# Two edits to the load queues of a decode kernel: x on ScalarE's queue, and W_down's last 96 rows in eight loads

## The chip, the core and the metric

The kernel runs on one core of one Trainium2 chip. The metric is the device time of one execution in microseconds (us). Three runs of the kernel before gave 670.46, 670.48 and 671.56; the median is 670.48. The profile and the trace are of a further execution, which took 671.36.

## The reference, cut to what matters

One new token per sequence, two sequences, model width 512. An attention block with a cache of 8192 positions and 32 heads of 128, then a gated feed-forward block of width 1376, each behind a layer norm and with a residual:

```
q      = layernorm(x) @ wq                       # x (2,1,512), wq (512, 4096)
scores = q . k_cache / sqrt(128)                 # k_cache (2, 32, 8192, 128), bf16
o      = softmax(scores) . v_cache
h      = x + o @ wo                              # wo (4096, 512)
gate, up = layernorm(h) @ W_gate, layernorm(h) @ W_up     # (512, 1376) each
out    = h + (relu(gate) * up) @ W_down          # W_down (1376, 512)
```

The two caches are 268 MB of the 281 MB that are read. Everything is read once.

## The kernel before, in words

**Steps.** The attention runs in N = 32 steps (line 108); a step is one sequence and two heads. Step i needs K(i) and V(i), 4 MB each (4096 KB in the profile), loaded by `load_kv` (lines 111 to 118). There are two buffers for K and two for V, so K(i) and K(i+2) share one, as do V(i) and V(i+2). In a step, TensorE transposes and multiplies a quarter of K (`scores_pe`, lines 248 to 278), VectorE multiplies the rest with q (`products`, line 286) and adds it up by halves (`scores`, lines 301 and 305), ScalarE takes the exponentials (line 320), and TensorE multiplies them with V one step later (`values`, line 336; `values_cols`, line 359, in the last two steps). `behind` normalises finished groups of heads and multiplies them with W_o.

**Order of the loads.** The order is the program's own (`tc.manual_schedule()`, line 138); no planner moves anything. All 85 loads and stores are issued by SyncE (SP), one after another: x (line 141), W_q (line 142), K(0) in four pieces, K(1), V(0) (lines 143 to 145), W_o in four pieces (lines 195 to 201), and then in the loop over steps (lines 413 to 444): K(i+2) as soon as `scores(i)` has read its buffer, V(i+1) as soon as `values(i-1)` has read its own. In step 8 (line 429) come three loads of W_down's last 96 rows, 64, 24 and 8 rows, into the last block of the tile `wd_sb`. In step 30 come W_gate, W_up and the rest of W_down (lines 435 to 444). So around line 432 SP's order is K(10), V(9), the W_down rows, K(11), V(10), K(12), V(11).

**What SP waits for.** Besides the buffers there is a second kind of wait, which no line of the kernel shows. The framework hands each load one of eight completion semaphores in turn, named DMAHW0 to DMAHW7 in the built program, and a load that gets a semaphore must wait until the load that had it before, eight loads earlier, has landed. Most of these waits are long fulfilled, or are those for the buffer anyway.

**Start.** x is cast by VectorE (line 168) and goes through a layer norm (`ln_cols`, lines 120 to 136) to `xn`; 128 small matmuls with W_q give q (line 176). ScalarE begins with loading an activation table and a warm-up activation (line 165).

**End.** After the last step come the residual (line 454), the second layer norm, gate and up (line 463), `hm` (line 473), the product with W_down, the last 96 rows first (line 478), and the store (line 484).

Of the kernel before, what the change touches and what calls it, by code (L numbers as in the profile page):

```python
# [13 lines left out]
def _free(t, offset, dims):  # L14

    return bass.AP(tensor=t.tensor, offset=t.offset + offset, ap=[t.ap[0]] + [list(d) for d in dims])


def _dram(t, offset, dims):
    return bass.AP(tensor=t.tensor, offset=t.offset + offset, ap=[list(d) for d in dims])  # L20
# [3 lines left out]
def kernel(  # L24
# [13 lines left out]
    nc = tc.nc  # L38
    P = nc.NUM_PARTITIONS
    B, Sq, D = A_x.shape  # L40
    _, Hkv, Sk, Dh = A_k_cache.shape
    Hq = A_wq.shape[1] // Dh
    F = B_W_gate.shape[1]
    KC = D // P
# [16 lines left out]
    FC = 11  # L61
# [17 lines left out]
    wd_sb = big.tile([P, FC, D], bf16)  # L79
# [31 lines left out]
    def load_kv(cache, buf, i, pieces=1):  # L111
        b, g = steps[i]
        w = ROW // pieces
        for k in range(pieces):
            nc.sync.dma_start(
                out=buf[:, i % 2, k * w:(k + 1) * w],
                in_=_dram(cache, (b * Hkv + 2 * g) * Sk * Dh + k * w, [[ROW, P], [1, w]]),
            )
# [19 lines left out]
    with tc.manual_schedule():  # L138

        xb = small.tile([P, B, KC], bf16, tag="xb")  # L140
        nc.sync.dma_start(out=xb, in_=_dram(A_x, 0, [[KC, P], [D, B], [1, KC]]))
        nc.sync.dma_start(out=wbig, in_=_dram(A_wq, 0, [[KC * Hq * Dh, P], [1, KC * Hq * Dh]]))
        load_kv(A_k_cache, kbuf, 0, pieces=4)
        load_kv(A_k_cache, kbuf, 1)
# [7 lines left out]
            out=nscale, in_=nscale, compare_op=ALU.not_equal, fill=-SCALE,  # L152
# [7 lines left out]
            out=pick, in_=pick, compare_op=ALU.not_equal, fill=1.0,  # L160
# [13 lines left out]
        for h in range(Hq):  # L174
            for c in range(KC):
                nc.tensor.matmul(  # L176
                    out=q_ps[:, h, :], lhsT=wq_sb[:, c, h * Dh:(h + 1) * Dh], rhs=xn[:, c, :],
# [4 lines left out]
        for b in range(B):  # L182
            for g0 in range(0, NG, 4):
                r_ps = ps2.tile([P, 4, Dh], f32, tag="tp")
                for k in range(4):
                    for j in range(2):
                        nc.tensor.matmul(
                            out=r_ps[j * HALF:(j + 1) * HALF, k, :],
# [6 lines left out]
        for h0, n in SETS:  # L195
            nc.sync.dma_start(
                out=wbig[:, h0 * D:(h0 + n) * D], in_=_dram(A_wo, h0 * Dh * D, [[n * D, P], [1, n * D]]),
            )
        nc.sync.dma_start(
            out=wo_sb[:, HM:Hq, :], in_=_dram(A_wo, HM * Dh * D, [[D, P], [Dh * D, Hq - HM], [1, D]]),  # L200
        )
        for (h0, n), qu, re in zip(SETS, quot, rest):
            nc.gpsimd.memset(re, 0.0)
            for k in range(P // n):
                nc.gpsimd.affine_select(  # L205
                    out=re, in_=re, compare_op=ALU.not_equal, fill=1.0,
# [4 lines left out]
                out=qu, in_=qu, compare_op=ALU.is_ge, fill=0.0,  # L211
# [3 lines left out]
                out=qu, in_=qu, compare_op=ALU.is_ge, fill=0.0,  # L215
# [32 lines left out]
        def scores_pe(i):  # L248
            b, g = steps[i]
            s = i % 2  # L250
            kt = kbuf[:, s, :]

            sc_ps = ps.tile([P, NPE, 2], f32, tag="sc")
            kT = small.tile([P, NPE * P], bf16, tag="kT")

            def times_q(c0):
                for k in range(TPC):
                    t = c0 + k
                    nc.tensor.matmul(  # L259
                        out=sc_ps[:, t, :], lhsT=kT[:, t * P:(t + 1) * P],  # L260
                        rhs=qT[:, b, 2 * g:2 * g + 2], start=True, stop=True,
                    )

            for c0 in range(0, NPE, TPC):
                t_ps = ps2.tile([P, TPC, P], bf16, tag="tp")
                for k in range(TPC):
                    t = NV + c0 + k
                    nc.tensor.transpose(t_ps[:, k, :], kt[:, t * Dh:(t + 1) * Dh], ident)  # L268
                nc.scalar.activation(  # L269
                    out=kT[:, c0 * P:(c0 + TPC) * P], in_=t_ps.rearrange("p t s -> p (t s)"), func=ACT.Copy,  # L270
                )
                if c0:
                    times_q(c0 - TPC)
            times_q(NPE - TPC)
            scol = small.tile([P, NT], f32, tag="scol")
            scols[i] = scol
            nc.scalar.activation(out=scol[0:HALF, NV:NT], in_=sc_ps[0:HALF, :, 0], func=ACT.Copy)  # L277
            nc.scalar.activation(out=scol[HALF:P, NV:NT], in_=sc_ps[HALF:P, :, 1], func=ACT.Copy)

        def products(i):  # L280

            b, g = steps[i]
            kt = kbuf[:, i % 2, :]
            for t0, n in ([(0, 32), (32, 32), (64, 32)] if i == 0 else [(0, NV)]):
                kv = _free(kt, t0 * Dh, [[Dh, n], [1, Dh]])
                nc.vector.tensor_tensor(  # L286
                    out=kv, in0=kv,
                    in1=_free(qrep, (b * NG + g) * Dh, [[0, n], [1, Dh]]), op=ALU.mult,
                )
# [37 lines left out]
        def values(i, part):  # L327

            b, g = steps[i]
            s = i % 2  # L330
            r = slice(32 * (g % 4), 32 * (g % 4) + 2 * VG)
            half = NT // VG // 2
            if part == 0:
                pv_ps[i] = ps2.tile([P, VG * Dh], f32, tag="o", name="pv_ps")
            for u in range(part * half, (part + 1) * half):
                nc.tensor.matmul(  # L336
                    out=pv_ps[i][r, :], lhsT=pgz[:, s, u].rearrange("p j t -> p (j t)"),
                    rhs=vbuf[:, s, u * VG * Dh:(u + 1) * VG * Dh], start=(u == 0), stop=(u == 2 * half - 1),
                )
            if part == 0:  # L340
                return
            w = (g // 4) % 2
            nc.scalar.activation(out=pv[r, w], in_=pv_ps[i][r, :], func=ACT.Copy)  # L343
            if i in groups:
                first, n = groups[i][1:]
                o_ps[i] = ps.tile([P, 8], f32, tag="of", name="o_ps")
                for t in range(VG):
                    nc.tensor.matmul(  # L348
                        out=o_ps[i][:, 0:2 * n], lhsT=pv[:, w, t * Dh:(t + 1) * Dh],
                        rhs=pick[:, t, first % 4:first % 4 + n].rearrange("p k j -> p (k j)"),  # L350
                        start=(t == 0), stop=(t == VG - 1),
                    )

        def values_cols(i):

            s = i % 2
            o_ps[i] = ps.tile([P, 8], f32, tag="of", name="o_ps")
            for t in range(NT):
                nc.tensor.matmul(  # L359
                    out=o_ps[i][:, 0:2], lhsT=vbuf[:, s, t * Dh:(t + 1) * Dh],  # L360
                    rhs=pgz[:, s, t // VG, :, t % VG], start=(t == 0), stop=(t == NT - 1),
                )
# [35 lines left out]
        def behind(i):  # L398

            if i not in groups:  # L400
                return
            sums(i)
            normalise(i)
            b, g0, n = groups[i]
            if b == B - 1:
                for k, (h0, m) in enumerate(SETS):
                    if 2 * (g0 + n) == h0 + m:
                        attend_set(k)
                if 2 * g0 >= HM:
                    for h in range(2 * g0, 2 * (g0 + n)):  # L410
                        attend(h)

        for i in range(N):
            scores_pe(i)
            products(i)
            if i >= 2:
                behind(i - 2)
            if 1 <= i < N - 1:
                values(i - 1, 0)
            if i == N - 1:  # L420
                values_cols(i - 1)
            scores(i)
            if i + 2 < N:
                load_kv(A_k_cache, kbuf, i + 2)
            if 1 <= i < N - 1:
                values(i - 1, 1)
            if i + 1 < N:
                load_kv(A_v_cache, vbuf, i + 1, pieces=4 if i + 1 == N - 1 else 1)
            if i == NG // 2:
                f0 = FSETS[-1][0]  # L430
                for p0, p1 in ((0, 64), (64, 88), (88, 96)):
                    nc.sync.dma_start(
                        out=wd_sb[p0:p1, FC - 1, :], in_=_dram(B_W_down, (f0 + p0) * D, [[D, p1 - p0], [1, D]]),
                    )
            if i == N - 2:
                for w, src in ((0, B_W_gate), (1, B_W_up)):
                    nc.sync.dma_start(
                        out=wgu[:, w], in_=_dram(src, 0, [[KC * F, P], [F, KC], [1, F]]),
                    )
                for f0, n, w in FSETS[:-1]:  # L440
                    nc.sync.dma_start(
                        out=wd_sb[0:w, f0 // P:f0 // P + n, :],
                        in_=_dram(B_W_down, f0 * D, [[n * D, w], [1, n * D]]),
                    )
# [15 lines left out]
        for k, w_ps in ((0, g_ps), (1, u_ps)):  # L460
            for fc, (f0, n, r, w) in enumerate(chunks):
                for c in range(KC):
                    nc.tensor.matmul(  # L463
                        out=w_ps[0:w, fc, :], lhsT=_free(wgu[:, k, c, :], f0 + r, [[n, w]]), rhs=hn[:, c, :],
# [10 lines left out]
        for k, fc in enumerate([FC - 1] + list(range(FC - 1))):  # L475
            w = chunks[fc][3]
            for c in range(KC):
                nc.tensor.matmul(  # L478
                    out=d_ps[:, c, :], lhsT=_free(wd_sb[0:w], fc * D + c, [[KC, P]]), rhs=hm[0:w, fc, :],
# [35 lines left out]
```

## Time and profile before

| | |
|---|---|
| runs before | 670.46, 670.48, 671.56 us; median 670.48 |
| the profiled execution's own time | 671.36 us |
| its span | 669.6 us |
| its mean granted TensorE clock | 0.784 |
| busy: PE, VectorE, ScalarE, GpSimd | 66%, 71%, 29%, 4% of the span |
| read from HBM | 281.05 MB, 420 GB/s over the span |

How to read it: the span goes from the first to the last instruction that the profiler recorded, and the execution takes 1.8 us more. "PE" is TensorE, "PEld" its weight loads, "DVE" VectorE, "ACT" ScalarE, "POOL" GpSimd, "SP" or "SPq" SyncE's queue. A load is shown where SP issues it; its landing shows where somebody who waited for it goes on. "DMA share" is the mean busy share of the core's 16 DMA engines; rounding of what lies across the edge of a stretch can take it a little over 1. An entry such as `[3.22 <-DMA kbuf<-in_A_k_cache_dram]` says that the engine sat idle 3.22 us before the instruction and that a landing load ended it.

### The profile page before, as it was taken

To read this page: it belongs to the slowest core of one execution; us is meant where nothing else is said; L and a number is where in the kernel's file an instruction comes from. 1 tells how busy PE (TensorE), PEld (TensorE's weight loads), DVE (VectorE), ACT (ScalarE), POOL (GpSimd) and SP (SyncE) were. 2 spreads that over 40 slices of the span, in tenths; PEclk is the share of its full clock that TensorE was granted. 3 is DMA by queue.
4 is the path that set the end of the run, shared out by engine and by line. 5 is a ranking of instruction groups with operands and counts; after the bars stand their busy time and mean duration, and the time that the engine had idled before them with its cause. 6 is when DMAs were issued, how large, how long until landed. Compare 5 with 4: busy or idle time off the path is not lost.

```text
span 669.6 us, 8843 instructions
## 1 busy us (share of the span) xinstructions
PE 444.4 (66%) x3878; PEld 230.3 (34%) x3878; DVE 478.5 (71%) x301; ACT 195.9 (29%) x372; POOL 26.2 (4%) x84
## 2 busy tenths in 40 slices
PE   2563765677666668776656776666776866588655
PEld 2432332333223333332323332333333433343255
DVE  1891788777778767778877776887777788777771
ACT  1531233333212333222233321323331223333130
POOL 7800000000000000000000000000000000000000
PEclk9857678988767788876789877778887767798775
DMA  8999999999999999999999999999999999999994
GB/s 349 433 419 428 437 436 426 431 428 430 437 424 430 415 434 426 439 426 432 428 430 432 431 434 422 435 430 430 430 431 434 428 426 431 438 430 426 427 412 167
DMA packets 12618, 281.62 MB, mean 421 GB/s; under 512 B 1860, under 2 KB 2468, under 8 KB 2980
## 3 DMA queue, kind: packets, MB, share of 16 engines
q1 hardware_dynamic: 12580, 281.06, 98.2%
q8 instruction: 30, 0.49, 0.3%
q14 instruction: 8, 0.07, 0.0%
HBM read 281.05 MB, written 0.00 MB: 420 GB/s over the span
## 4 chain that ended last, share of the span: by engine, by line
DMA 67%; PE 21%; DVE 10%; ACT 1%; issue 0%; SPq 0%; DVEq 0%
DMA vbuf<-in_A_v_cache_dram 53%; PE pv_ps L336 18%; DMA kbuf<-in_A_k_cache_dram 12%; DVE kbuf L301 5%; DVE kbuf L286 4%; DMA wbig<-in_A_wq_dram 2%; PE mx_ps L312 1%; DVE scol L305 1%; ACT kT L269 1%; PE q_ps L176 1%; PE o_ps L359 1%; PE g_ps L463 0%; PE d_ps L478 0%; PE u_ps L463 0%; PE z_ps L236 0%
## 5 line engine op out<-in xcount | busy, mean ns | idle before, releaser
L336 PE MATMUL pv_ps<-vbuf,pgz 128*8 128x512 bf16 x960 | 281.9, 460 | 122.1 <-DMA vbuf<-in_A_v_cache_dram 122.1
L286 DVE TENSOR_TENSOR kbuf<-kbuf,qrep 128x12288 bf16<-128x12288 bf16 (+1 forms) x34 | 210.0, 6181 | 119.7 <-DMA kbuf<-in_A_k_cache_dram 106.7
L301 DVE TENSOR_TENSOR kbuf<-kbuf 128x6144 bf16<-128x6144 bf16 (+3 forms) x128 | 212.1, 1657 | 4.2
L336 PEld LDWEIGHTS <-pgz 128*8 128x8 bf16 x960 | 93.3, 100 | 286.7 <-issue 215.6
L269 ACT ACTIVATE kT<-t_ps 128x1024 bf16<-128x1024 bf16 x128 | 124.2, 1021 | 32.4 <-PE t_ps L268 32.0
L320 ACT ACTIVATE pgz<-scol,nm 64x128 bf16<-64x128 f32 x64 | 25.5, 399 | 327.6 <-DVE nm L317 326.9
L268 PE MATMUL t_ps<-ident,kbuf 128*128 128x128 bf16 x1024 | 77.4, 227 | 16.9 <-DMA kbuf<-in_A_k_cache_dram 16.9
L259 PE MATMUL sc_ps<-qT,kT 128*128 128x2 bf16 x1024 | 45.4, 165 | 48.3 <-ACT kT L269 45.5
L268 PEld LDWEIGHTS <-kbuf 128*128 128x128 bf16 x1024 | 62.4, 102 | 27.4 <-DMA kbuf<-in_A_k_cache_dram 25.6
L259 PEld LDWEIGHTS <-kT 128*128 128x128 bf16 x1024 | 34.7, 97 | 67.5 <-ACT kT L269 67.5
L317 DVE TENSOR_REDUCE nm<-mx_ps 128x2 f32<-128x128 f32 x32 | 9.3, 292 | 39.8 <-PE mx_ps L312 39.8
L343 ACT ACTIVATE pv<-pv_ps 8x512 f32<-8x512 f32 x30 | 17.7, 589 | 64.6 <-PE pv_ps L336 64.6
L305 DVE TENSOR_REDUCE scol<-kbuf 128x96 f32<-128x768 bf16 x32 | 30.5, 953 | 1.1
L312 PE MATMUL mx_ps<-nscale,pm 128*128 128x128 f32 x64 | 16.2, 336 | 7.0 <-DVE pm L310 6.9
L312 PEld LDWEIGHTS mx_ps<-nscale,pm 128*128 128x128 f32 x64 | 9.9, 194 | 20.3 <-issue 11.7
L205 POOL TENSOR_SCALAR_AFFINE_SELECT rest<-rest 128x4 bf16<-128x4 bf16 (+2 forms) x56 | 16.7, 299 | 4.0 <-POOL rest L205 0.2
L348 PE MATMUL o_ps<-pick,pv 128*128 128x8 f32 (+1 forms) x64 | 8.4, 258 | 5.5 <-ACT pv L343 5.5
L320 ACT ACTIVATION_READ_ACCUMULATOR pgz<-scol,nm 64x1 f32 x64 | 11.8, 185 | 0.0
L310 DVE TENSOR_REDUCE pm<-scol 128x1 f32<-128x128 f32 x32 | 9.2, 286 | 3.3
L348 PEld LDWEIGHTS o_ps<-pick,pv 128*128 128x128 f32 x64 | 7.7, 191 | 9.5 <-ACT pv L343 8.3
L277 ACT ACTIVATE scol<-sc_ps 64x32 f32<-64x32 f32 x32 | 6.1, 191 | 14.3 <-PE sc_ps L259 14.3
L176 PE MATMUL q_ps<-xn,wbig 128*128 128x2 bf16 x128 | 3.6, 165 | 8.7 <-DMA wbig<-in_A_wq_dram 8.7
(71 smaller groups left out, 94.5 us busy)
## 6 DMA issues: line engine op xcount, KB each, us to landing
kbuf<-in_A_k_cache_dram SPq DMA_DIRECT2D x31, 4096.0 KB, 24.6
vbuf<-in_A_v_cache_dram SPq DMA_DIRECT2D x31, 4096.0 KB, 29.3
wbig<-in_A_wq_dram SPq DMA_DIRECT2D x1, 4096.0 KB, 12.9
kbuf<-in_A_k_cache_dram SPq DMA_DIRECT2D x4, 1024.0 KB, 18.2
vbuf<-in_A_v_cache_dram SPq DMA_DIRECT2D x4, 1024.0 KB, 18.5
wbig<-in_A_wo_dram SPq DMA_DIRECT2D x1, 2048.0 KB
kbuf<-in_B_W_gate_dram SPq DMA_DIRECT2D x1, 1376.0 KB
kbuf<-in_B_W_up_dram SPq DMA_DIRECT2D x1, 1376.0 KB
```

The lines of the kernel that those rows point to most:

```text
L205: nc.gpsimd.affine_select(out=re, in_=re, compare_op=ALU.not_equal, fill=1.0, base=-k * n, pattern=[[-1, n]], channel_multiplier=1,)
L259: nc.tensor.matmul(out=sc_ps[:, t, :], lhsT=kT[:, t * P:(t + 1) * P], rhs=qT[:, b, 2 * g:2 * g + 2], start=True, stop=True,)
L268: nc.tensor.transpose(t_ps[:, k, :], kt[:, t * Dh:(t + 1) * Dh], ident)
L269: nc.scalar.activation(out=kT[:, c0 * P:(c0 + TPC) * P], in_=t_ps.rearrange("p t s -> p (t s)"), func=ACT.Copy,)
L286: nc.vector.tensor_tensor(out=kv, in0=kv, in1=_free(qrep, (b * NG + g) * Dh, [[0, n], [1, Dh]]), op=ALU.mult,)
L301: nc.vector.tensor_tensor(out=lo, in0=lo, in1=_free(kt, half, [[Dh, NV], [1, half]]), op=ALU.add,)
L305: nc.vector.tensor_reduce(out=scol[:, 0:NV], in_=_free(kt, 0, [[Dh, NV], [1, 8]]), axis=AXIS.X, op=ALU.add,)
L312: nc.tensor.matmul(out=mx_ps.rearrange("p a b -> p (a b)"), lhsT=_free(pm, 0, [[0, P]]), rhs=nscale, start=True, stop=True,)
L320: nc.scalar.activation(out=pgz[r, s, :, j, :], in_=scol[r, :].rearrange("p (u t) -> p u t", t=VG), func=ACT.Exp, scale=SCALE, bias=nm[r, j ...
L336: nc.tensor.matmul(out=pv_ps[i][r, :], lhsT=pgz[:, s, u].rearrange("p j t -> p (j t)"), rhs=vbuf[:, s, u * VG * Dh:(u + 1) * VG * Dh], sta ...
L343: nc.scalar.activation(out=pv[r, w], in_=pv_ps[i][r, :], func=ACT.Copy)
L348: nc.tensor.matmul(out=o_ps[i][:, 0:2 * n], lhsT=pv[:, w, t * Dh:(t + 1) * Dh], rhs=pick[:, t, first % 4:first % 4 + n].rearrange("p k j - ...
```

## The change

x is issued by ScalarE's queue, ahead of the activation table load, so that W_q is the first load that SP issues. W_down's last 96 rows are loaded by eight loads in place of three: load c takes rows c, c + 8, c + 16 and so on, twelve rows, into the twelve partitions of the same numbers. The bytes and their places are the same.

```diff
@@ -138,7 +138,7 @@
         xb = small.tile([P, B, KC], bf16, tag="xb")
-        nc.sync.dma_start(out=xb, in_=_dram(A_x, 0, [[KC, P], [D, B], [1, KC]]))
+        nc.scalar.dma_start(out=xb, in_=_dram(A_x, 0, [[KC, P], [D, B], [1, KC]]))
         nc.sync.dma_start(out=wbig, in_=_dram(A_wq, 0, [[KC * Hq * Dh, P], [1, KC * Hq * Dh]]))
@@ -428,9 +428,9 @@
             if i == NG // 2:
                 f0 = FSETS[-1][0]
-                for p0, p1 in ((0, 64), (64, 88), (88, 96)):
+                for c in range(8):
                     nc.sync.dma_start(
-                        out=wd_sb[p0:p1, FC - 1, :], in_=_dram(B_W_down, (f0 + p0) * D, [[D, p1 - p0], [1, D]]),
+                        out=wd_sb[c:F - f0:8, FC - 1, :], in_=_dram(B_W_down, (f0 + c) * D, [[8 * D, (F - f0) // 8], [1, D]]),
                     )
```

In the instruction lists of the two built programs, TensorE, VectorE and GpSimd have the same instructions in the same order. ScalarE has one more, the load of x, as its first. SP has one less at the start and five more at line 432, with these waits in the program after:

```
25 L115 DMACopy kbuf<-in_A_k_cache_dram 128x16384 [waits DMAHW0_49,DVE_49,PE_49]
26 L115 DMACopy vbuf<-in_A_v_cache_dram 128x16384 [waits DMAHW1_49,PE_49]
27 L432 DMACopy wd_sb<-in_B_W_down_dram 12x512 x4
28 L432 DMACopy wd_sb<-in_B_W_down_dram 12x512 [waits DMAHW2_49]
29 L432 DMACopy wd_sb<-in_B_W_down_dram 12x512 [waits DMAHW3_49]
30 L432 DMACopy wd_sb<-in_B_W_down_dram 12x512 [waits DMAHW4_49]
31 L432 DMACopy wd_sb<-in_B_W_down_dram 12x512 [waits DMAHW5_49]
32 L115 DMACopy kbuf<-in_A_k_cache_dram 128x16384 [waits DMAHW6_49,DVE_49,PE_49]
```

In the program before, the three loads of line 432 have no wait.

## The prediction, made before the change was run

> **What bounds the kernel now.** First the page's strip of slices and the summary of the chain that ended last:
>
> ```profile
> DMA  8999999999999999999999999999999999999994
> GB/s 349 433 419 428 437 436 426 431 428 430 437 424 430 415 434 426 439 426 432 428 430 432 431 434 422 435 430 430 430 431 434 428 426 431 438 430 426 427 412 167
> ...
> DMA 67%; PE 21%; DVE 10%; ACT 1%; issue 0%; SPq 0%; DVEq 0%
> ```
>
> The DMA engines are busy in every slice between the first and the last, at about 430 GB/s; PE (66%) and DVE (71%) are not. So the stream of loads is the bound: what starts the stream earlier comes off the end, and what makes a hole in it is put on the end. A 4 MB load (4096 KB) takes 4.194 MB / 430 GB/s = 9.75 us, a step two of them, 19.5.
>
> A hole opens only if SP issues the next load after everything issued before has gone through. So next SP's instructions in order of time, and the stretch of the chain around line 432:
>
> ```profile
> 195.70 0.33 SPq L115 DMA_DIRECT2D kbuf<-in_A_k_cache_dram  x1
> 201.00 0.33 SPq L115 DMA_DIRECT2D vbuf<-in_A_v_cache_dram  x1
> 201.37 1.51 SPq L432 DMA_DIRECT2D wd_sb<-in_B_W_down_dram  x3
> 215.86 0.36 SPq L115 DMA_DIRECT2D kbuf<-in_A_k_cache_dram  x1
> 221.58 0.35 SPq L115 DMA_DIRECT2D vbuf<-in_A_v_cache_dram  x1
> 235.67 0.33 SPq L115 DMA_DIRECT2D kbuf<-in_A_k_cache_dram  x1
> ```
>
> ```profile
> 201.00 30.43 DMA vbuf<-in_A_v_cache_dram
> 231.43 0.04 issue
> 231.47 6.22 PE pv_ps L336 x16
> ```
>
> These are K(10), V(9), the three W_down loads, K(11), V(10), K(12). V(9) is issued at 201.00 and lands at 231.43; K(11) is issued at 215.86, 15.6 us before that, and waits its turn in the queue. That lead is the whole cover of the stream. VectorE's rows show when K(10) and K(11) landed (221.3 and 241.6):
>
> ```profile
> 221.29 6.56 DVE L286 TENSOR_TENSOR kbuf<-kbuf,qrep 128x12288 bf16<-128x12288 bf16 x1 [2.95 <-DMA kbuf<-in_A_k_cache_dram]
> 241.66 6.56 DVE L286 TENSOR_TENSOR kbuf<-kbuf,qrep 128x12288 bf16<-128x12288 bf16 x1 [3.22 <-DMA kbuf<-in_A_k_cache_dram]
> ```
>
> **Edit 1, x on ScalarE's queue.** The chain begins:
>
> ```profile
> 0.80 0.44 SPq L141
> 1.25 0.06 issue
> 1.30 12.92 DMA wbig<-in_A_wq_dram
> ```
>
> W_q can be issued at 0.80 in place of 1.30, so the stream may start up to 0.50 us earlier. The 2 KB of x still go through the same 16 DMA engines, now beside W_q; the worst is that they cost W_q as much as they cost SP, 0.44, so the gain lies between 0.06 and 0.50. I take 0.45, since 2 KB is little work. On ScalarE the issue (0.44) is put before the table load of 0.80; the warm-up activation behind it waits 2.12 us for POOL, which hides it. x itself may come later: it is cast at 2.68, `xn` is ready at 6.48, 3.8 us on, and is needed when W_q lands at 14.22. x may therefore land up to about 10 without moving q, against 2.68 now. If it came with W_q, q would be some 4 us late; what waits behind q is W_o at 17.82 and, through step 0, K(2) at 34.01, while the queue holds W_q, K(0), K(1), V(0) until about 13.7 + 3 x 9.75 = 43, and W_o for 9.75 more. Four us stay hidden; past about 19 they would show.
> The Trainium skill, "DMA: Bandwidth & Descriptors", section "Queues, rings and completion order", says that each DMA engine takes turns between the queues it has work for, a packet at a time; by it x's tiny pieces could stand behind long pieces of W_q and land late. No run shown has loads on two of these queues at once. By the rule the sum is the same as long as x is less than 19 us late.
>
> **Edit 2, eight loads in place of three.** The bytes are the same, 96 KB (0.2 us of the stream). Five more issues at 0.28 to 0.59 (the three L432 issues are 0.585, 0.547, 0.277) are 1.4 to 2.9 us of SP, ahead of K(11), with 13 us free there: nothing. The Trainium skill's table "Rules for kernel authors" in the same page speaks against the edit: coalesce small transfers, below 64 KB one pays mostly overhead, with about 2.0 us fixed per DMA by its fit; five more paid one by one would be 10 us. The three loads here were issued within 1.51 us of each other, so that is not the price I count.
>
> What I do count is the eight completion semaphores. In the instruction list the fifth to eighth load wait on DMAHW2 to DMAHW5, the loads eight places before: K(9), V(8), K(10), V(9). The trace already has this kind of wait. The W_down loads of line 441 fill space nobody reads before, and yet SP waits there for V(30) and the first piece of V(31), eight places earlier:
>
> ```profile
> SPq L441 <- DMA vbuf<-in_A_v_cache_dram: 9.7, 2, 7.4
> ```
>
> K(9) has landed by 200.8 and V(8) by 211.7, K(10) at 221.3; but V(9) lands at 231.43, and SP works in order. So the eighth load holds K(11) and V(10) behind it until the queue has just run empty. Step by step, from V(9)'s landing: 231.43 - 0.45 (edit 1) + 0.04 (reaction, as PE's) + 0.50 (issue of the eighth load) + 0.05, so K(11) is issued at 231.57 instead of 215.86. How long a 4 MB load takes into an idle queue the trace shows once, W_q: 12.92 from issue to landing, 3.2 over 9.75; the 2 KB store at the end, 3.0 from issue to landing, says the same of the latency. K(11) lands at 231.57 + 12.92 = 244.5 instead of 241.6: **2.9 us later, edit 1 included**. V(10) is issued right behind it (its buffer is free at 221.6), K(12) when `scores(10)` ends, 235.67, so there is no second hole. Nothing gives the time back: DVE needs 15 us of a 19.5 us step and waits on each K.
>
> Bounds of this term. Low: gain 0.50, eighth issue 0.28, restart 9.55 (439 GB/s, the best slice) + 3.0 = 12.55, K(11) at 243.8, +2.2. High: gain 0, issue 0.59, and one of the instruction fetches falls on the slowest DMA engine in the hole's load: 30 fetches at 0.3% of 16 engines' span are 1.07 us each; K(11) at 246.1, +4.5. I take W_q's row, which is nearest in size.
> A second unknown is lag between the DMA engines. At the end they do not stop together:
>
> ```profile
> 654.00:656.00 2.00, 2.00 (x81) 2.00 (x78) 0.00 (x0) 0.00 (x0) 0.00 (x0) 0.50 1.01 418
> 656.00:658.00 2.00, 1.32 (x23) 1.09 (x19) 0.46 (x3) 0.00 (x0) 0.00 (x0) 0.50 0.79 318
> 658.00:660.00 2.00, 0.59 (x2) 0.53 (x3) 0.85 (x6) 0.30 (x1) 0.00 (x0) 0.50 0.53 210
> 660.00:662.00 2.00, 1.93 (x56) 1.92 (x56) 0.02 (x1) 0.20 (x2) 0.00 (x0) 0.50 0.40 161
> 662.00:664.00 2.00, 1.60 (x46) 1.54 (x44) 0.24 (x2) 0.04 (x1) 0.00 (x0) 0.50 0.15 52
> ```
>
> The column before last is the DMA share: engines end over some 7 us. A hole lets all start again together, so the lag that the slowest had by 231 is lost with it; the sum above, landing against landing, already has that at K(11), and what the slowest engine at the end lost may be 0.5 less or 1 more.
>
> **Sum.** The profiled execution took 671.36: 671.36 + 2.9 = 674.3. It is 0.9 over the median of the runs shown, from which the sum is 673.4. I forecast the middle, **673.9**.
>
> **Rivals.**
> - *No hole.* If the eighth load's semaphore were last held by K(10), one place further back, SP would be free at 221.3 and issue K(11) 10 us before the queue is empty. Then only edit 1 is left: 671.4 or 670.5 less 0.06 to 0.5, about 670.5, not slower. It decides by which load the eighth waits for: one that lands before about 229 costs nothing. The count in SP's list speaks for V(9); the list names only a semaphore. 7%.
> - *A larger hole* (+4.5 to +6.5): the engines that had little lag at 231 set the end, so that they lose the whole time since they ran dry at about 227.5, not since 231. For it: DMA share falls to 0.91 in 228 to 230. Against it: engines that lag late probably lagged early. About 676.5. 10%.
> - *x starves* behind W_q and K(0): over 19 us late, step 0 holds up K(2) and makes a hole at 53. Two 4 MB loads' time must pass first. 676 or more. 2%.
> - *A smaller hole* (+1.3 to +2), if the restart takes less than W_q's did: 672.3. 7%; another 2% for gains I don't see, over 0.2%.
>
> The forecast (+2 to +4.5) has 72%. **Range** 672.2 to 675.9: 670.48 + 2.2, with 0.5 off for lag, to 671.36 + 4.5. A difference under 0.2%, 1.3 us, is about what this kernel's measurement cannot tell from none. Slower by over that: forecast, larger hole, starving and nearly all of the smaller, 0.90; within: no hole and a rest, 0.08; faster 0.02.
>
> **What would show it.** In SP's waits, a new L432 row on vbuf with one wait of about 10 us, and one of about 10 on kbuf; K(11)'s issue at about 231.5 instead of 215.9; DMA share near 0 between about 231 and 233; DVE's L286 of step 11 about 3 us later than 241.66 and every later one as well; W_q's issue at 0.80. K(11) issued before 229 would make it wrong, as would an L286 of step 31 at 633 in spite of a hole.

## The result, and the profile after

The kernel after takes 673.88 us (median of six runs, 673.59 to 674.95) against 670.58 for the kernel before on the same chip (six runs, 670.46 to 671.56): a ratio of 1.0047, 95% interval 1.0036 to 1.0058. That is 3.3 us slower. The profiled execution took 674.27, 2.9 more than that of before (671.36); its span is 672.5.

The page's strip of slices shows where the time went, in one place:

```profile
DMA  8999999999999799999999999999999999999994
GB/s 361 443 407 439 435 426 428 422 437 432 433 426 432 297 433 434 435 426 424 433 432 430 429 430 430 433 430 430 429 432 428 432 428 431 432 432 430 427 410 196
```

Slice 14 (a slice is 16.8 us, so 219 to 235) has 297 GB/s where its neighbours have 432; before, no inner slice was under 412. The 135 GB/s that are missing, over 16.8 us and divided by 430, are 5.3 us of the stream at its mean rate. The end came only 3.3 us later; that the DMA engines which ran dry first lost more than those that set the landings would explain the difference, but no view here shows single engines. Busy times of the compute engines barely moved (DVE 71%, PE 66%).

SP's instructions around line 432 in the kernel after, in order of time; they stand for the same loads as in the prediction's fence, with eight small ones in place of three:

```profile
195.22 0.33 SPq L115 DMA_DIRECT2D kbuf<-in_A_k_cache_dram  x1
200.50 0.33 SPq L115 DMA_DIRECT2D vbuf<-in_A_v_cache_dram  x1
200.88 30.61 SPq L432 DMA_DIRECT2D wd_sb<-in_B_W_down_dram  x8
231.61 0.45 SPq L115 DMA_DIRECT2D kbuf<-in_A_k_cache_dram  x1
232.15 1.31 SPq L115 DMA_DIRECT2D vbuf<-in_A_v_cache_dram  x1
235.24 0.33 SPq L115 DMA_DIRECT2D kbuf<-in_A_k_cache_dram  x1
```

The row `x8` merges eight issues and the waits between them: SP stands in line 432 from 200.88 to 231.49. K(11) goes out at 231.61 instead of 215.86. The eighth issue on its own:

```profile
230.77 0.72 SPq L432 DMA_DIRECT2D wd_sb<-in_B_W_down_dram  x1
```

The chain of the kernel after, and VectorE's rows for K(10) and K(11):

```profile
200.50 30.25 DMA vbuf<-in_A_v_cache_dram
230.75 0.04 issue
230.80 6.29 PE pv_ps L336 x16
```

```profile
220.86 6.56 DVE L286 TENSOR_TENSOR kbuf<-kbuf,qrep 128x12288 bf16<-128x12288 bf16 x1 [3.00 <-DMA kbuf<-in_A_k_cache_dram]
244.16 6.56 DVE L286 TENSOR_TENSOR kbuf<-kbuf,qrep 128x12288 bf16<-128x12288 bf16 x1 [6.33 <-DMA kbuf<-in_A_k_cache_dram]
```

V(9) lands at 230.75, 0.7 earlier than before; K(11) is used at 244.16, 2.5 later; and VectorE's wait for it grew from 3.22 to 6.33. SP's own waits have two new rows on line 432, and one on line 196:

```profile
SPq L432 <- DMA vbuf<-in_A_v_cache_dram: 15.6, 2, 9.2
SPq L196 <- DMA xb<-in_A_x_dram: 11.4, 1, 11.4
...
SPq L432 <- DMA kbuf<-in_A_k_cache_dram: 8.8, 1, 8.8
```

The longest of each, 8.8 on K(10) and 9.2 on V(9), come one behind the other; the other 6.4 on vbuf are the sixth load's wait for V(8). The row of line 196 is the same kind of wait: W_o's first piece is eight places behind x. The DMA share (the column before last) in the stretches around:

```profile
226.00:228.00 2.00, 0.00 (x0) 0.00 (x0) 1.97 (x2) 0.36 (x2) 0.00 (x0) 0.50 0.77 313
228.00:230.00 2.00, 0.00 (x0) 0.00 (x0) 2.00 (x1) 0.00 (x0) 0.00 (x0) 0.50 0.12 41
230.00:231.00 1.00, 0.20 (x1) 0.08 (x1) 0.96 (x2) 0.00 (x0) 0.00 (x0) 0.50 0.00 0
231.00:232.00 1.00, 1.00 (x3) 0.26 (x2) 1.00 (x1) 0.00 (x0) 0.00 (x0) 0.50 0.06 16
232.00:233.00 1.00, 1.00 (x4) 0.37 (x3) 0.97 (x2) 0.00 (x0) 0.00 (x0) 0.50 1.35 373
```

The queue runs empty around 228; from 229 or so to 232 next to nothing moves, though V(9)'s landing shows only at 230.75. In the kernel before the share was 0.91 from 228 to 230 and 0.92 from 230 to 232.

### The profile page after: what moved, and what is told of

Its sections match the earlier page's. It is cut to its first block, busy times and chain, and to the rows that moved or that the text cites. A ratio compares the mean times of both kernels' runs of the same rounds, so it can differ in the third digit from the quotient of the medians.

```text
span 672.5 us, 8849 instructions
## 1 busy us (share of the span) xinstructions
PE 446.3 (66%) x3878; PEld 231.7 (34%) x3878; DVE 477.6 (71%) x301; ACT 195.9 (29%) x372; POOL 15.6 (2%) x84
## 4 chain that ended last, share of the span: by engine, by line
DMA 67%; PE 25%; DVE 4%; POOL 2%; ACT 1%; issue 1%; POOLq 0%; SPq 0%; DVEq 0%
DMA vbuf<-in_A_v_cache_dram 67%; PE pv_ps L336 21%; DVE kbuf L301 2%; POOL rest L205 1%; PE mx_ps L312 1%; DVE kbuf L286 1%; ACT kT L269 1%; PE q_ps L176 1%; PE o_ps L359 1%; DVE scol L305 0%; PE g_ps L463 0%; PE d_ps L478 0%; PE u_ps L463 0%; PE z_ps L236 0%; PE v_ps L131 0%
## 5 line engine op out<-in xcount | busy, mean ns | idle before, releaser
L168 DVE CAST xc<-xb 128x8 f32<-128x8 bf16 x1 | 0.2, 172 | 15.8 <-DMA xb<-in_A_x_dram 15.8
L205 POOL TENSOR_SCALAR_AFFINE_SELECT rest<-rest 128x4 bf16<-128x4 bf16 (+2 forms) x56 | 10.7, 191 | 4.0 <-POOL rest L205 0.2
```

The lines of the kernel that those rows point to most:

```text
L205: nc.gpsimd.affine_select(out=re, in_=re, compare_op=ALU.not_equal, fill=1.0, base=-k * n, pattern=[[-1, n]], channel_multiplier=1,)
```

## The experiments

The theory: in a row of loads, each waits until the load eight places earlier has landed, so that eight small loads behind V(9) hold K(11) until V(9) has landed and the queue is empty. The rivals: every small load has a price; the spacing of the rows has one; the late x does it. Ratios are to the kernel before, measured beside it on the same chip, with 95% intervals; the first four ran on one chip, the next four on another, the last two again together.

### Edit 1 alone

```diff
-        nc.sync.dma_start(out=xb, ...)
+        nc.scalar.dma_start(out=xb, ...)
```

> Edit 1 alone: x on ScalarE's queue, W_down's last 96 rows in three loads as before. Theory (the semaphore wait of the eighth load makes the hole): x lands at about 15.8 and q is about 4.7 us late, as in the kernel after, but the queue is 20 us ahead there, so nothing shows; W_q starts 0.5 earlier: 670.1, ratio 0.9993, and K(11) issued near 215.4. Rival (the late x is what costs): 673.5 or more.

670.29 against 671.11, ratio 0.9990 (0.9981 to 0.9999). The late x costs nothing, although it is late: VectorE's cast, first of the kernel before, then of this one,

```profile
2.68 0.89 DVE L168 CAST xc<-xb 128x8 f32<-128x8 bf16 x1 [2.68 <-DMA xb<-in_A_x_dram]
```

```profile
15.96 0.17 DVE L168 CAST xc<-xb 128x8 f32<-128x8 bf16 x1 [15.96 <-DMA xb<-in_A_x_dram]
```

shows x 13 us later. SP's K(2), which step 0 holds up, is issued at 38.80 instead of 34.01, still well before the queue would be empty (about 53 by the prediction's sum). The gain is between 0.1 and 1.3 us; the half us expected lies in it.

### Edit 2 alone

The kernel after, with x on SyncE's queue as before.

> Edit 2 alone: the eight loads of twelve rows, x on SyncE's queue as before. Theory: the whole loss and half a us more than with both edits, 674.3, ratio 1.0055, DMA share near 0 for a us or two after V(9) has landed, at about 231.4. Rival (the late x costs): 670.6.

675.19 against 671.11, ratio 1.0056 (1.0042 to 1.0070), +4.1, which is 0.6 to 0.8 more than with both edits, where half a us more was expected. The whole loss is edit 2's. DMA share is 0.01 from 230 to 232, and K(11) is issued at 232.21.

### Six loads, and seven

Six loads, against the kernel after:

```diff
-                for c in range(8):
+                for c in range(6):
                     nc.sync.dma_start(
-                        out=wd_sb[c:F - f0:8, FC - 1, :], in_=_dram(B_W_down, (f0 + c) * D, [[8 * D, (F - f0) // 8], [1, D]]),
+                        out=wd_sb[c:F - f0:6, FC - 1, :], in_=_dram(B_W_down, (f0 + c) * D, [[6 * D, (F - f0) // 6], [1, D]]),
```

Seven:

```diff
-                for c in range(8):
+                for p0, p1, st in [(c, 72, 6) for c in range(6)] + [(72, 96, 1)]:
                     nc.sync.dma_start(
-                        out=wd_sb[c:F - f0:8, FC - 1, :], in_=_dram(B_W_down, (f0 + c) * D, [[8 * D, (F - f0) // 8], [1, D]]),
+                        out=wd_sb[p0:p1:st, FC - 1, :], in_=_dram(B_W_down, (f0 + p0) * D, [[st * D, (p1 - p0 + st - 1) // st], [1, D]]),
```

> Both edits, but six loads of sixteen rows spaced by six. The sixth waits for V(8), K(11) for K(10) (landed near 221), and V(10) for V(9), when K(11) is already moving. Theory: no hole, 670.1, as edit 1 alone; K(11) issued near 221. Rival (each added small load has its price): three of the five added loads, 60% of the loss, 672.1. Rival (spaced rows cost): the whole loss, 673.9.

> Both edits, but seven loads: six of twelve rows spaced by six, and the last 24 rows together. No small load waits for V(9), but K(11) is then eight places behind V(9) and waits for it itself. Theory: the same hole as with eight, less the half us of the eighth issue: 673.5. Rival (each added small load has its price): four of the five, 80% of the loss, 672.9, and no step between six and seven loads. Rival (the eighth small load alone is what waits): 670.1.

Six: 670.04 against 671.11, ratio 0.9985 (0.9976 to 0.9994). Seven: 673.38, ratio 1.0028 (1.0016 to 1.0039). Between six loads and seven lie 3.3 us, between three and six nothing. SP's instructions of the kernel with six:

```profile
201.07 10.99 SPq L432 DMA_DIRECT2D wd_sb<-in_B_W_down_dram  x6
221.17 0.33 SPq L115 DMA_DIRECT2D kbuf<-in_A_k_cache_dram  x1
231.35 0.33 SPq L115 DMA_DIRECT2D vbuf<-in_A_v_cache_dram  x1
```

and of the kernel with seven:

```profile
200.24 21.23 SPq L432 DMA_DIRECT2D wd_sb<-in_B_W_down_dram  x7
231.19 0.35 SPq L115 DMA_DIRECT2D kbuf<-in_A_k_cache_dram  x1
231.64 0.37 SPq L115 DMA_DIRECT2D vbuf<-in_A_v_cache_dram  x1
```

With six, SP also waits, 11 us in line 432 and then for K(10) and V(9), but K(11) goes out at 221.17, ten us before V(9) is through, and V(10) finds K(11) on its way: the waits cost nothing. With seven, the small loads are through by 221.5, and it is K(11) itself, now the eighth behind V(9), that waits until 231.19. So it is a place in the order, not the small load, that pays. A price for each load would have put six at 672.1.

### Eight loads with neighbouring rows

```diff
-                        out=wd_sb[c:F - f0:8, FC - 1, :], in_=_dram(B_W_down, (f0 + c) * D, [[8 * D, (F - f0) // 8], [1, D]]),
+                        out=wd_sb[12 * c:12 * c + 12, FC - 1, :], in_=_dram(B_W_down, (f0 + 12 * c) * D, [[D, 12], [1, D]]),
```

> Both edits, but each of the eight loads takes twelve neighbouring rows into twelve neighbouring partitions. Theory (the number of loads in a row decides): as the kernel after, 673.9. Rival (the spacing of rows and partitions costs): 670.1.

672.88 against 671.04, ratio 1.0026 (1.0016 to 1.0036): between the two expectations. The hole is there (K(11) issued at 231.07, DMA share 0.00 from 230 to 231), but the loss is smaller than the kernel after's. So both were run again, beside each other on one chip.

> The kernel after once more, beside the one with neighbouring rows on the same chip. That one came out at a ratio of 1.0026 and the kernel after at 1.0047, but not in the same call. Theory (the number of loads decides, and the hole's size scatters by what the DMA engines' lag gives back): both within half a us of each other. Rival (the spacing of the rows has a price of its own): the kernel after slower by 1.0 to 1.4 us again.

> Eight loads of twelve neighbouring rows, with both edits, once more. Theory: 673.5, within half a us of the kernel after. Rival (spacing costs): 672.7, 1.0 to 1.4 below the kernel after.

Kernel after: 674.53, ratio 1.0054 (1.0040 to 1.0067). Neighbouring rows: 673.01, ratio 1.0033 (1.0022 to 1.0045). The second was 1.5 lower; by the ratios the first pair was 1.4 apart. Here the ends of the two intervals overlap a little, but both pairs fall the same way, so the theory that the number alone decides is too simple: with a hole open, the spacing has a price of 1 to 1.5 us. Part of it is in the eighth issue, which stands in the open hole. SP's rows of the kernel after, run again,

```profile
230.72 0.72 SPq L432 DMA_DIRECT2D wd_sb<-in_B_W_down_dram  x1
231.56 0.44 SPq L115 DMA_DIRECT2D kbuf<-in_A_k_cache_dram  x1
232.10 1.55 SPq L115 DMA_DIRECT2D vbuf<-in_A_v_cache_dram  x1
```

and of the one with neighbouring rows, run again:

```profile
230.71 0.30 SPq L432 DMA_DIRECT2D wd_sb<-in_B_W_down_dram  x1
231.12 0.36 SPq L115 DMA_DIRECT2D kbuf<-in_A_k_cache_dram  x1
231.57 0.38 SPq L115 DMA_DIRECT2D vbuf<-in_A_v_cache_dram  x1
```

Twelve spaced partitions take SP 0.72 to issue (0.71 to 0.89 over all eight), twelve neighbouring ones 0.30 (to 0.44). K(11) goes out 0.44 later, and VectorE's last `products` starts 0.2 later here (635.97 against 635.73) and 0.55 later in the first pair (636.13 against 635.58). The profiled executions differ by 0.8 here and by 1.4 in the first pair; what these starts do not hold of it arises after them, in step 31 and the end, and why is open. From that row to `y` (line 483, the last VectorE instruction) the profiles of kernels without a hole scatter from 30.9 to 32.1, so one profile of each does not settle it.

### Four and four

```diff
-            if i == NG // 2:
+            if i in (NG // 2, NG // 2 + 4):
                 f0 = FSETS[-1][0]
-                for c in range(8):
+                for c in range(4) if i == NG // 2 else range(4, 8):
```

> Both edits, the eight loads of twelve spaced rows unchanged, but four of them in step 8 and four in step 12. Nothing issued is then eight places behind a load that has not landed when its turn comes. Theory: no hole, 670.1. Rival (each small load has its price): the whole loss, 673.9.

670.36 against 671.04, ratio 0.9993 (0.9984 to 1.0002). The same eight loads, spaced and slow to issue (3.20 for four), come without the loss, for K(11) is issued at 214.65:

```profile
199.83 3.20 SPq L432 DMA_DIRECT2D wd_sb<-in_B_W_down_dram  x4
214.65 0.34 SPq L115 DMA_DIRECT2D kbuf<-in_A_k_cache_dram  x1
221.76 0.33 SPq L115 DMA_DIRECT2D vbuf<-in_A_v_cache_dram  x1
```

### The eight loads twice

```diff
-            if i == NG // 2:
+            if i in (NG // 2, NG // 2 + 4):
```

The second time it loads the same rows into the same place.

> Both edits, and the eight loads are issued a second time in step 12, the same rows into the same place. Theory: a second hole of the same make, in step 12 near 312: 3.4 over the kernel after from landing to landing, less what the engines' lag gives back there, 677.0. Rival (a small load's price): eight more of them at 0.7 each, 679.3. Rival (the loss happens once, for instance because the hole only brings the engines level): 674.1.

678.52 against 671.04, ratio 1.0110 (1.0096 to 1.0123): +7.5 where one set gave +3.3 and +3.5. SP's waits double, and so does the hole; the second one in the windows view:

```profile
SPq L432 <- DMA vbuf<-in_A_v_cache_dram: 30.3, 4, 9.2
SPq L432 <- DMA kbuf<-in_A_k_cache_dram: 17.9, 2, 9.0
```

```profile
312.00:314.00 2.00, 0.46 (x2) 0.16 (x2) 1.97 (x2) 0.00 (x0) 0.00 (x0) 0.50 0.03 10
```

The second hole costs 4.0 to 4.2. The theory had put it at 3.1 and the price for small loads at 5.4, so the time alone lies about halfway and does not decide between them; the second empty stretch in the trace, and the four and four above without a loss, do. Why the second hole is larger than the first is open.

### One load

```diff
-                for c in range(8):
+                for p0, p1 in ((0, 96),):
                     nc.sync.dma_start(
-                        out=wd_sb[c:F - f0:8, FC - 1, :], in_=_dram(B_W_down, (f0 + c) * D, [[8 * D, (F - f0) // 8], [1, D]]),
+                        out=wd_sb[p0:p1, FC - 1, :], in_=_dram(B_W_down, (f0 + p0) * D, [[D, p1 - p0], [1, D]]),
```

> Edit 1, and the 96 rows in a single load. Theory: 670.0 to 670.1, no different from three loads, since two waits fewer were never on the path; the best version in sight. Rival (each small load has its price of 0.7): 668.7.

670.45 against 671.04, ratio 0.9992 (0.9983 to 1.0000). One load, three, six, or four and four, with x on ScalarE's queue: 0.6 to 1.1 below the kernel before, and not to be told apart.

## Why the prediction was right, step by step

- **Bound.** The stream of loads is the bound: a hole in it reached the end. K(11) is 2.5 later than before, `products` of step 31 is 2.5 later, the profiled execution 2.9. The rows of step 31, first of the kernel before, then of the kernel after:

```profile
633.64 6.56 DVE L286 TENSOR_TENSOR kbuf<-kbuf,qrep 128x12288 bf16<-128x12288 bf16 x1 [2.71 <-DMA kbuf<-in_A_k_cache_dram]
```

```profile
636.13 6.56 DVE L286 TENSOR_TENSOR kbuf<-kbuf,qrep 128x12288 bf16<-128x12288 bf16 x1 [2.51 <-DMA kbuf<-in_A_k_cache_dram]
```

- **Edit 1.** W_q is issued at 0.80, as forecast; the gain taken was 0.45, and edit 1 alone gave 0.8, interval 0.1 to 1.3, which does not settle its size. That x may land much later was right, and by more than the case named (landing with W_q, at about 14): x landed at 15.8, so that q starts at 18.98 instead of 14.27, and W_o and K(2) go out 4.7 later. "Four us stay hidden" held. x lands at 15.8 to 16.4 in every kernel that has it on the second queue, and at 2.7 in both that have not. The transfer records in the trace of the kernel after show why: x's 256 pieces of 8 bytes start in sixteen batches of sixteen, the first eight 1.21 to 1.33 us apart, the last eight 0.21 to 0.32, and one 32 KB piece of W_q takes 1.21, one 8 KB piece of K(0) 0.31 (medians). So one piece of x goes out for each big piece. The Trainium skill says in "DMA: Bandwidth & Descriptors", "Queues, rings and completion order", that each DMA engine takes turns between its queues a packet at a time; the trace agrees that they take turns, and here a turn is a single piece.
- **Edit 2, small loads.** No price for five more issues while SP has time: six loads and four and four show it. The estimate of 10 us, which the prediction set aside, came from the Trainium skill, "DMA: Bandwidth & Descriptors": the advice to coalesce in "Rules for kernel authors", with the page's fit of about 2.0 us fixed per DMA. That fit is for loads that GpSimd issues. SyncE's small loads, issued while the queue was full, show no such price: four and four is at a ratio of 0.9993 (0.9984 to 1.0002).
- **Edit 2, the wait.** The eighth load waits for V(9), as counted: it was issued at 230.77, V(9) landed at 230.75. That this is the program's semaphore, and not a limit on how many loads the queue takes, rests on the instruction list, where the waits stand; no run used another number of semaphores. The rival "no hole" fell with it, and a price for each small load fell as well: the loss is absent with six loads and with four and four, and comes twice where the row of eight comes twice. x was 13 us late, under the 19 of the rival "x starves". Two of the signs came otherwise than told: SP waits on vbuf twice in line 432, since V(8) held up the sixth load as well, and the DMA share is near 0 from about 229 to 232, not from 231 to 233, because the queue ran dry before V(9)'s landing showed.
- **The sum.** K(11)'s issue was put at 231.57 and came at 231.61, from two errors that cancel: V(9) landed 0.68 earlier, not 0.45, and the eighth issue took 0.72, over the 0.59 that was the upper bound. That bound came from loads of neighbouring partitions. From K(11)'s issue to its use were 12.55, not 12.92, so W_q's row overstated the restart by 0.4 here; in the profiles of the other runs with a hole in step 8 the same stretch is 12.35 to 13.53. K(11) came 2.5 late, not 2.9. The end made up for it: 2.9 in the profiles, of which the tail behind step 31 gave 0.4, within the scatter of that tail; and 3.3 in the medians. That the forecast of 673.9 and the median of 673.88 agree so closely is therefore luck: the forecast was the middle of two sums 0.9 apart, and terms of half a us cancelled. What the runs confirm is the mechanism and the range.
- **Lag.** "What the slowest engine at the end lost may be 0.5 less or 1 more": no lag is seen given back, K(11) and step 31 are late by the same 2.5. With edit 2 alone they are late by the same 4.1.

## What to carry to other kernels

When a framework hands loads a few completion semaphores in turn, a burst of small loads spends the lead of the big ones: no load can be issued before the one a whole round earlier has landed, whatever buffers are free. Count places in the queue, not bytes: six small loads were free here, and the seventh cost 3.3 us. Where a stream of loads is the bound, ask of each wait whether the queue still holds work when it ends, since here waits of 9 us cost nothing with that cover, and a wait of 9 us that ended with the queue empty cost 1.8 to 4.1 us.

## What was not expected of the hardware

A load into twelve partitions eight apart took SP 0.71 to 0.89 us to issue, one into twelve neighbouring partitions 0.30 to 0.44, with the same bytes. With the queue full that cost nothing (four and four). And 2 KB of x on the second queue, issued at the same moment as W_q, landed 13 us later than alone ahead of it, one piece for each big piece of the other queue.
